# Expert products with phi, placed at the seam between a retention layer and two mixture-of-experts layers

## The chip, the cores and the metric

The kernel runs on one core of a Trainium2 chip. The metric is the device time of one execution in microseconds (us); lower is better. The engines are named as in the profile: PE multiplies matrices (PEld loads its weights), DVE, ACT and POOL work on vectors, and SP issues most of the transfers between the chip's memory (DRAM) and the on-chip memory (SBUF). Each engine works through its own instructions in order; semaphores tie them together. PE writes its results to PSUM, which has few banks.

## The reference

Three layers in float32. q, k and v have 4 batches, 8 heads, 768 steps and 64 columns, so the token matrix x is 3072 x 512.

```python
def _attn_ref(q, k, v):                       # retention
    for t in range(S):
        state = gamma * state + einsum('bhd,bhe->bhde', k[:, :, t], v[:, :, t])
        y[:, :, t] = scale * einsum('bhd,bhde->bhe', q[:, :, t], state)

def _moe_ref(x, w_gate, w_output_gate, w1, w2):   # each token goes to one of 8 experts
    e_idx = argmax(x @ w_gate, axis=1)
    for e in range(8):
        h = maximum(x[mask] @ w1[e], 0.0)
        out[mask] = gate_w[mask, None] * eom[mask, e, None] * (h @ w2[e])

def _moe2_ref(x, phi, w1, w2):                # 32 slots, 4 for each of 8 experts
    logits = x @ phi
    d = softmax(logits, axis=0)
    slot_input = d.T @ x
    slot_out[e] = maximum(slot_input[e] @ w1[e], 0.0) @ w2[e]
    return softmax(logits, axis=1) @ slot_out
```

## The kernel before

**Retention** goes over 24 tiles of 128 tokens (NTILE = 24), in steps i = 0 to 25. A step of the loop runs a fixed list of small stages, ORDER, in which each stage works on tile i, i-1 or i-2; the order of the list is the order of the instructions on every engine. It ends with the gate of each token: `run` counts tokens by expert, `count()` (step 25) sorts the experts by size into `ordi`, R0 to R4 and `im` (the tiles pa, pb and place_mm) place each token in its expert's list, and after the last step DVE makes from it `xidx`, the row numbers for gathering tokens, and `limi`, which says whether an expert has more tokens than its room. The scaled rows of x are written to DRAM as `xs`, 128 rows in a step.

**The products with phi.** The second layer needs only (h @ w2) @ phi of the first one's output for its logits, so w2 @ phi is made ahead for each expert: `wq(e)` multiplies the transposed second weight by phi. It has 16 matmuls, four (g = 0..3) for each of four k-quarters kk; the four of a quarter write 32 rows each of one PSUM bank. DVE transposes the bank into `ws`, and ACT's queue writes it to DRAM as `wps[e]`. The weights come in 32 loads `wt` of 512 KB on SP's queue (`wq_load`). A table, WAT, says in which step of retention the stage `wp` does which expert: 0 to 4 in steps 6, 10, 14, 18 and 22, and 5 in step 25 (NTILE + 1). Experts 6 and 7 follow after the last step, behind `limi` and the first `gather`. All use the one PSUM bank `xn`, which x's transposes use too.

**The block for left-over tokens.** All five engines read `limi` (line 632) and skip the block at line 739 if no expert overflows, as in this case. SBUF of retention and of this block is given to the experts' pools after it.

**The experts.** They come in order of size; "expert 0" is the first of them. `gather(e)` fetches its tokens (C[0] = 448 for expert 0, in tiles of 128 rows, XT) by four indirect transfers on POOL. `x_mm` transposes them on PE, for each k-quarter kk all token tiles; `x_split` makes of each quarter a rounded part xh (ACT) and the rest xl (DVE). `split_w(g)` does the same with the first weights (wh, wl), which `load_w(g)` loads as `r`. `l1(g)` is one of 8 column groups of an expert: 12 matmuls `hps`, then a relu on ACT. `behind(e - 1, f)` spreads the rest of the expert before over the groups. `logits(e, hf)` multiplies relu tiles by wps (loaded as `wp` by `load_wp`), its first half after group f = 4. `keep_warm` multiplies a tile by itself; nothing reads the result. `load_m2` fills a pool, `m2p`, with weights of the second layer, one tile of 256 KB in each group from the fifth on.

Of the kernel before, what the change touches and what calls it, by code (L numbers as in the profile page):

```python
# [9 lines left out]
F32 = mybir.dt.float32  # L10
# [12 lines left out]
E = 8  # L23
# [13 lines left out]
WAT = {6: 0, 10: 1, 14: 2, 18: 3, 22: 4, NTILE + 1: 5}  # L37
# [94 lines left out]
def retention_moe_kernel(ctx, tc, qt, kt, kn, vn, gates, moe_w1, moe_w2,  # L132
# [124 lines left out]
    with ExitStack() as pa:  # L257
# [43 lines left out]
        def wq(e):  # L301

            ps = pT.tile([128, 512], F32, tag="xn", name="wpsum")
            for kk in range(KD):
                t = wtt.pop((e, kk))
                for g in range(4):
                    nc.tensor.matmul(out=ps[32 * g:32 * g + 32, 0:256], lhsT=phi[:, kk, :], rhs=t[:, 256 * g:256 * g + 256],
                                     start=(kk == 0), stop=(kk == KD - 1), skip_group_check=True)
            ws = sc2.tile([128, KF, NS], F32, tag="ws", name="ws")
            nc.vector.transpose(out=ws, in_=ps[:, 0:256].rearrange("p (b t) -> p b t", t=32))  # L310
            nc.scalar.dma_start(out=wps[e].rearrange("p (f s) -> p f s", s=NS), in_=ws)

# [228 lines left out]
        def place_add(i):  # L541
# [11 lines left out]
            "oq": out_state, "os": out_scores, "st": state, "wp": lambda i: wq(WAT[i]) if i in WAT else None,  # L553
# [41 lines left out]
        for i in range(NTILE + 2):  # L595
            load(i + 3)
            load_dq(i + 2)
            if i == NTILE + 1:
                count()
            for n in ORDER:  # L600
                step[n](i)
            if i == 0:
                late_tables()
            for u in range(4 * E):
                if i == (1 + u if u < 20 else 21 + (u - 20) // 3):
                    wq_load(*divmod(u, 4))

        full = [128, E, 4, E]
# [14 lines left out]
        for e in range(6, E):  # L623
            wq(e)
# [126 lines left out]
    with ExitStack() as pb:  # L751
# [5 lines left out]
        xh, xl, hs, hB, wp, w2n, lps, lrs, lrs2, sms, lms, ces, gps, gsb, gts, slo = ({} for _ in range(16))  # L757
        puts = {}

        def x_mm(e, kk, pool=None, tag="x"):  # L760
            ps = (pool or ps_x).tile([128, C[e]], F32, tag=tag, name="xps")
            for j, r in enumerate(XT[e]):
                nc.tensor.transpose(out=ps[:, j * 128:j * 128 + r], in_=xg[e][j][0:r, kk * 128:(kk + 1) * 128],  # L763
                                    identity=ident[0:r, 0:r])
            return ps
# [10 lines left out]
        def keep_warm(w, n, pool, tag):  # L776

            ps = pool.tile([128, DM], F32, tag=tag, name="warm")
            for _ in range(n):
                nc.tensor.matmul(out=ps[:, 0:w.shape[1]], lhsT=w[:, 0:128], rhs=w, start=True, stop=True)  # L780
# [16 lines left out]
        def h_tr(e, f):  # L797

            c = C[e]
            if f == 0:  # L800
                hB[e] = hbp.tile([128, NBX, KF, 32], F32, tag="hB", name="hB")
            nc.vector.transpose(out=hB[e][:, 0:NB[e], f, :], in_=hs[e * KF + f][:, 0:c].rearrange("p (b t) -> p b t", t=32))  # L802

# [162 lines left out]
        split_w(1)  # L966
        keep_warm(w1_t[0][0], NW0, ps_h, "h")
        for kk, ps in enumerate([x_mm(0, kk, *((ps_x, "x") if kk < 2 else (ps_1, "lr"[kk - 2]))) for kk in range(KD)]):
            x_split(0, ps)
        for g in range(G):  # L970
            e, f = divmod(g, KF)
            if f == 0:
                if e + 1 < E:
                    gather(e + 1)
                load_er(e + 2)
                load_wp(e)
# [20 lines left out]
            if f == 4:  # L997
                logits(e, 0)
                mask(e)
# [215 lines left out]
```

## Time and profile before

| | us |
|---|---|
| median of 3 runs | 479.92 (477.62 to 480.44) |
| the profiled execution, its run | 484.3 |
| its span, first to last instruction | 482.5 |
| PE busy | 426.3 (88% of the span) |
| DVE busy | 279.4 (58%) |
| ACT busy | 165.8 (34%) |
| POOL busy | 110.1 (23%) |

The profile comes from one execution. Its times count from the span's start. Retention lasts to about 150, the experts run from about 159 to 395, and the second layer's own weights fill the rest. A busy PE is not always a PE at its peak, since matmuls overlap.

### The profile page before, as it was taken

What the parts mean: (1) busy time and instruction counts of PE and PEld (TensorE: products, weight loads), DVE (VectorE), ACT (ScalarE), POOL (GpSimd) and SP (SyncE); (2) the same over time, 40 slices, a digit from 0 to 9 for tenths busy, and PEclk for the clock granted to TensorE, in tenths of its full rate; (3) what the DMA queues carried; (4) which work ended last, traced back from release to release, by engine and by line L of the source; (5) the groups of instructions that cost most, each with busy time, mean ns of one, the idle gap of its engine ahead of it and who ended that gap; (6) DMA issues with size and microseconds to landing.
All of it is one profiled execution on the core that took longest, in us unless ns stands there. A gap on an engine that the chain in (4) does not pass through costs nothing.

```text
span 482.5 us, 12772 instructions
## 1 busy us (share of the span) xinstructions
PE 426.3 (88%) x4811; PEld 326.3 (68%) x4811; DVE 279.4 (58%) x964; ACT 165.8 (34%) x418; POOL 110.1 (23%) x113
## 2 busy tenths in 40 slices
PE   3899999989974799999999999998979989798874
PEld 3676777767742588876786778867767776425754
DVE  1797989888883326655555465654646636321433
ACT  1243334333340344534333344333343432110342
POOL 1712021211003311315133161241502112020040
PEclk9999999999999599999999999999999999989995
DMA  8999898898788457828839569397593945999998
GB/s 272 398 358 355 291 390 300 326 401 313 282 311 283 113 177 230 274 69 303 282 114 300 199 214 326 103 323 246 180 322 114 321 165 156 379 382 365 386 392 273
DMA packets 65176, 132.54 MB, mean 275 GB/s; under 512 B 8435, under 2 KB 16625, under 8 KB 65105
## 3 DMA queue, kind: packets, MB, share of 16 engines
q1 hardware_dynamic: 56848, 118.30, 70.0%
q0 software_dynamic: 3600, 9.05, 5.4%
q10 hardware_dynamic: 4656, 4.29, 2.7%
q8 instruction: 39, 0.64, 0.6%
q14 instruction: 33, 0.26, 0.2%
HBM read 117.58 MB, written 14.05 MB: 273 GB/s over the span
## 4 chain that ended last, share of the span: by engine, by line
PE 36%; DMA 13%; DVE 8%; issue 4%; ACT 3%; another core or an unknown queue 2%; ACTq 1%; SPq 0%; DVEq 0%
PE hps L790 16%; DMA r<-in_moe_w_dram 8%; PE gps L899 4%; DMA m<-in_moe_w_dram 3%; PE gsum L914 3%; DVE hB L802 2%; PE slo L923 2%; PE xps L763 2%; DVE wl L226 2%; PE lps L821 2%; PE fh L1057 2%; PE so L1107 2%; DVE xl L772 1%; ACT wh L225 1%
## 5 line engine op out<-in xcount | busy, mean ns | idle before, releaser
L790 PE MATMUL hps<-xh,wh 128*128 128x416 f32 (+2 forms) x256 | 96.1, 376 | 0.6 <-issue 0.6
L790 PE MATMUL hps<-xl,wh 128*128 128x416 f32 (+2 forms) x256 | 89.9, 351 | 0.7 <-issue 0.6
L790 PE MATMUL hps<-xh,wl 128*128 128x416 f32 (+2 forms) x256 | 89.5, 350 | 0.0
L226 DVE TENSOR_TENSOR wl<-r,wh 128x512 fp32r<-128x512 f32 x64 | 43.5, 680 | 55.9 <-ACT wh L225 52.1
L790 PEld LDWEIGHTS hps<-xh,wh 128*128 128x128 f32 x256 | 48.7, 190 | 14.8 <-issue 13.2
L795 ACT ACTIVATE h<-hps 128x416 f32<-128x416 f32 (+2 forms) x64 | 32.6, 509 | 74.3 <-PE hps L790 48.9
L225 ACT ACTIVATE wh<-r 128x512 fp32r<-128x512 f32 x64 | 40.3, 631 | 43.4 <-DMA r<-in_moe_w_dram 27.4
L790 PEld LDWEIGHTS hps<-xl,wh 128*128 128x128 f32 x256 | 48.9, 191 | 3.1 <-issue 2.1
L790 PEld LDWEIGHTS hps<-xh,wl 128*128 128x128 f32 x256 | 48.7, 190 | 1.2 <-issue 0.4
L882 POOL DMA_INDIRECT ctok<-cn,xidx x29 | 28.7, 990 | 88.3 <-DVE cn L879 81.9
L214 POOL DMA_INDIRECT xg<-xs,xidx x29 | 30.6, 1055 | 69.2 <-DMA wps<-ws 33.3
L346 POOL TENSOR_TENSOR k<-vk,cs 128x512 f32<-128x512 f32 x20 | 22.4, 1122 | 84.0 <-DMA vk<-in_vn_dram 48.3
L373 DVE TENSOR_TENSOR sS<-s,csa 128x512 f32<-128x512 f32 x48 | 30.7, 681 | 9.7 <-DMA csa<-in_consts_dram 8.1
L802 DVE STREAM_TRANSPOSE hB<-h 128x416 f32<-128x416 f32 (+2 forms) x64 | 34.3, 577 | 0.0
L830 POOL TENSOR_SCALAR lm<-cs,rt 128x416 f32<-128x416 f32 (+2 forms) x8 | 16.2, 2024 | 76.7 <-DVE srun L855 76.6
L363 PE MATMUL s<-qk 64*128 64x128 f32 x384 | 29.0, 292 | 4.3 <-DMA qk<-in_qt_dram 4.3
L363 PEld LDWEIGHTS s<-qk 64*128 64x128 f32 x384 | 24.3, 194 | 8.3 <-DMA qk<-in_qt_dram 4.3
L772 DVE TENSOR_TENSOR xl<-xps,xh 128x416 fp32r<-128x416 f32 (+2 forms) x32 | 18.3, 582 | 17.7 <-issue 8.7
L406 PE MATMUL o<-sS,vk 128*64 128x128 f32 x384 | 27.2, 281 | 0.2 <-DVE sS L373 0.2
L481 ACT ACTIVATE sm<-sm 128x8 f32<-128x8 f32 x24 | 5.1, 211 | 64.1 <-DVE sm L469 64.1
L899 PE MATMUL gps<-hB,pT 32*32 32x256 f32 x816 | 19.1, 384 | 8.4 <-DVE pT L853 8.4
L771 ACT ACTIVATE xh<-xps 128x416 fp32r<-128x416 f32 (+2 forms) x32 | 16.2, 513 | 19.2 <-PE hps L790 11.0
(155 smaller groups left out, 691.8 us busy)
## 6 DMA issues: line engine op xcount, KB each, us to landing
m<-in_moe_w_dram SPq DMA_DIRECT2D x128, 256.0 KB
wt<-in_moe_w_dram SPq DMA_DIRECT2D x32, 512.0 KB
r<-in_moe_w_dram SPq DMA_DIRECT2D x64, 256.0 KB
w<-in_moe_w_dram SPq DMA_DIRECT2D x64, 256.0 KB
vk<-in_vn_dram SPq DMA_DIRECT2D x12, 512.0 KB
qk<-in_kt_dram SPq DMA_DIRECT2D x12, 512.0 KB
xs<-xnat SPq DMA_DIRECT2D x24, 256.0 KB
qk<-in_qt_dram SPq DMA_DIRECT2D x11, 512.0 KB
```

The lines of the kernel that those rows point to most:

```text
L214: nc.gpsimd.indirect_dma_start(out=xg[e][j][0:r, :], out_offset=None, in_=xs[:, :], in_offset=bass.IndirectOffsetOnAxis(ap=xidx[0:r, e, j: ...
L225: nc.scalar.activation(out=hi, in_=t, func=ACTF.Copy)
L226: nc.vector.tensor_tensor(out=lo, in0=t, in1=hi, op=ALU.subtract)
L363: nc.tensor.matmul(out=ps[h][:, p, :], lhsT=raw["kt", i][r, p, :], rhs=raw["qt", i][r, p, :], start=True, stop=True, tile_position=(64 * h ...
L373: nc.vector.tensor_tensor(out=sS[i][:, :, h, :], in0=sps.pop((i, h)), in1=con("dm", 128).rearrange("p (a b) t -> p a b t", b=2)[:, :, h, : ...
L406: nc.tensor.matmul(out=o_at(i, p, h), lhsT=vv[:, 2 * p + h, :], rhs=s[:, p, h, :], start=(c == 0 and p < 2), stop=True, skip_group_check=True)
L772: nc.vector.tensor_tensor(out=lo[:, 0:c], in0=ps, in1=hi[:, 0:c], op=ALU.subtract)
L790: nc.tensor.matmul(out=ps, lhsT=a[:, kk * 128:(kk + 1) * 128], rhs=x[e][kk][:, 0:c], start=(n == 0), stop=(n == 11))
L795: nc.scalar.activation(out=hs[g][:, 0:c], in_=ps, func=ACTF.Relu)
L802: nc.vector.transpose(out=hB[e][:, 0:NB[e], f, :], in_=hs[e * KF + f][:, 0:c].rearrange("p (b t) -> p b t", t=32))
L882: put = nc.gpsimd.indirect_dma_start(out=ctok[:, :], out_offset=bass.IndirectOffsetOnAxis(ap=xidx[0:r, e, j:j + 1], axis=0), in_=cn[0:r, j ...
L899: nc.tensor.matmul(out=ps[a][32 * c:32 * c + 32, :], lhsT=pT_[q, b, :], rhs=hB[e][q, b].rearrange("p f t -> p (f t)"), start=(b < 4), stop ...
```

## The change

The products with phi of experts 5, 6 and 7 (the sixth to the eighth) move, and some work at the start of expert 0 is put in another order:

- Expert 5 is done in step 24, not 25. `wq` is split into `wq_mm` (matmuls) and `wq_put` (transpose and write). Expert 6 has its first two quarters in step 25, in a bank of the scores' tag `s`, its other two after the loop, and `wq_put(6)` after `limi` and the gather.
- Expert 7 is done in expert 0 of the first layer: eight loads of 256 KB go into the first tiles of `m2p` at its start, `phi_mm(0)` to `phi_mm(3)`, four matmuls each, follow the groups f = 1 to 4, and the last one transposes and writes.
- `load_wp(0)` is put behind `phi_mm(3)`, and `logits(0, 0)` and `mask(0)` after group 6 instead of 4.
- The `wt` loads of step 21 on come earlier by a step or so: two in step 20, three each in 21 and 22, none later.
- At the start of expert 0 `keep_warm` goes, x is transposed by token tile (all four quarters of a tile, then the next tile), and `split_w(1)` comes between x's second and third quarter.

```diff
-WAT = {6: 0, 10: 1, 14: 2, 18: 3, 22: 4, NTILE + 1: 5}
+WAT = {6: 0, 10: 1, 14: 2, 18: 3, 22: 4, NTILE: 5}
...
+        def wq(i):
+            if i in WAT:
+                wq_mm(WAT[i])
+                wq_put(WAT[i])
+            elif i == NTILE + 1:
+                wq_mm(6, range(2), "s")
...
-            for u in range(4 * E):
-                if i == (1 + u if u < 20 else 21 + (u - 20) // 3):
+            for u in range(4 * E - 4):
+                if i == (1 + u if u < 20 else 20 + (u - 19) // 3):
                     wq_load(*divmod(u, 4))
 
+        wq_mm(6, range(2, KD))
...
         gather(0)
-        for e in range(6, E):
-            wq(e)
+        wq_put(6)
...
+        def load_wt(kk):
+            for hf in range(2):
+                u = 2 * kk + hf
+                wtt[u] = m2p.tile([128, 512], F32, tag="m2", name="wt")
+                nc.sync.dma_start(out=wtt[u], in_=moe_w2[1, E - 1, kk * 32:(kk + 1) * 32, :].rearrange("a (b h f) -> (a b) h f", h=2, f=512)[:, hf])
+
+        def phi_mm(kk):
+
+            if kk == 0:
+                wpp[0] = ps_x.tile([128, 512], F32, tag="x", name="wpp")
+            for g in range(4):
+                nc.tensor.matmul(out=wpp[0][32 * g:32 * g + 32, 0:256], lhsT=phi[:, kk, :],
+                                 rhs=wtt[2 * kk + g // 2][:, 256 * (g % 2):256 * (g % 2) + 256],
+                                 start=(kk == 0), stop=(kk == KD - 1), skip_group_check=True)
+            if kk == KD - 1:
+                ws = sp.tile([128, KF, NS], F32, tag="wp", name="ws", bufs=2)
+                nc.vector.transpose(out=ws, in_=wpp[0][:, 0:256].rearrange("p (b t) -> p b t", t=32))
+                nc.scalar.dma_start(out=wps[E - 1].rearrange("p (f s) -> p f s", s=NS), in_=ws)
...
         split_w(0)
-        split_w(1)
-        keep_warm(w1_t[0][0], NW0, ps_h, "h")
-        for kk, ps in enumerate([x_mm(0, kk, *((ps_x, "x") if kk < 2 else (ps_1, "lr"[kk - 2]))) for kk in range(KD)]):
+        for kk in range(KD):
+            load_wt(kk)
+        xps = [(ps_x if kk < 2 else ps_1).tile([128, C[0]], F32, tag="xxlr"[kk], name="xps") for kk in range(KD)]
+        for j in range(len(XT[0])):
+            for kk in range(KD):
+                x_turn(0, kk, j, xps[kk])
+        for kk, ps in enumerate(xps):
             x_split(0, ps)
+            if kk == 1:
+                split_w(1)
...
-                load_wp(e)
+                if e:
+                    load_wp(e)
...
+            if e == 0 and 0 < f <= KD:
+                phi_mm(f - 1)
+                if f == KD:
+                    load_wp(0)
-            if f == 4:
+            if f == (4 if e else 6):
                 logits(e, 0)
                 mask(e)
```

PE in retention's steps 24 and 25 before, from the place search of step 24 (pb and pa) to the last products (wpsum); cp is the count, g the gate's bank:

```order
L538 MATMUL g<-pb,pa 128x32
L456 MATMUL xn<-cs_65,xT 128x128 x4
L569 LDWEIGHTS ones
L569 MATMUL cp<-run,ones 128x8
L502 LDWEIGHTS tri
L502 MATMUL g<-oh,tri 128x8
L503 LDWEIGHTS ones
L503 MATMUL g<-run,ones 128x8
L307 MATMUL wpsum<-wt,phi 32x256 x16
L538 MATMUL g<-pb,pa 128x32
L307 MATMUL wpsum<-wt,phi 32x256 x32
```

The same place now:

```order
L310 MATMUL wpsum<-wt,phi 32x256 x16
L551 MATMUL g<-pb,pa 128x32
L469 MATMUL xn<-cs_65,xT 128x128 x4
L582 LDWEIGHTS ones
L582 MATMUL cp<-run,ones 128x8
L515 LDWEIGHTS tri
L515 MATMUL g<-oh,tri 128x8
L516 LDWEIGHTS ones
L516 MATMUL g<-run,ones 128x8
L310 MATMUL wpsum<-wt,phi 32x256 x8
L551 MATMUL g<-pb,pa 128x32
L310 MATMUL wpsum<-wt,phi 32x256 x8
```

Expert 5's sixteen products stand a step earlier, ahead of step 24's place search; expert 6's stand in two halves around that of step 25; expert 7's are gone from here.

SP's queue at the start of the experts before (ordi is the number of an expert, wp the read of wps, r the first weights):

```order
L201 TENSOR_LOAD ordi
L201 ISA x2
L201 TENSOR_LOAD ordi
L201 ISA x2
L806 ISA
L806 DMA wp<-wps 128x256
L208 ISA
L208 DMA r_4494<-in_moe_w_dram 128x512
```

The same place now:

```order
L201 TENSOR_LOAD ordi
L201 ISA x2
L824 DMA wt<-in_moe_w_dram 128x512 x8
L201 TENSOR_LOAD ordi
L201 ISA x2
L208 ISA
L208 DMA r_4477<-in_moe_w_dram 128x512
```

And further on, where wp went, around the first load of the second layer's weights (m):

```order
L208 ISA
L208 DMA r_4574<-in_moe_w_dram 128x512
L246 DMA m_4576<-in_moe_w_dram 128x512
L841 ISA
L841 DMA wp<-wps 128x256
L208 ISA
L208 DMA r_4606<-in_moe_w_dram 128x512
L246 DMA m_4608<-in_moe_w_dram 128x512
```

The read wp left the head of the queue and stands behind the fifth r load of expert 0 and the first m; the eight wt loads stand at the head.

## Rows read from the trace of the kernel before

**Rows 1.** Chain of waits, 138 to 172: start us, us, what.
```profile
158.56 0.64 ACT wh L225
...
159.25 1.22 PE warm L780 x2
160.47 4.32 PE xps L763 x16
164.79 7.25 PE hps L790 x23
```

**Rows 2.** Windows around the seam: stretch, busy by engine, clock, DMA share, GB/s.
```profile
156.30:164.70 8.40, 5.46 (x18) 3.39 (x18) 2.97 (x5) 2.79 (x5) 0.36 (x1) 0.50 0.39 119
164.70:169.90 5.20, 5.20 (x15) 4.62 (x15) 1.42 (x3) 1.36 (x3) 4.13 (x5) 0.50 0.61 173
169.90:179.60 9.70, 9.70 (x48) 8.55 (x46) 2.77 (x4) 3.96 (x8) 1.23 (x1) 1.00 0.48 161
```

**Rows 3.** The tile limi: duration in ns min/median/max, first and last start.
```profile
L632 PEldq TENSOR_LOAD <-limi x1: 733/733/733, 151.3 to 151.3; - x1
...
L632 ACTq TENSOR_LOAD <-limi x1: 473/473/473, 153.7 to 153.7; - x1
```

**Rows 4.** Timeline, steps 24 and 25: start, us, engine, what, idle before and releaser.
```profile
139.07 0.69 ACT L495 ACTIVATE xnat<-xn,sm 128x512 f32<-128x512 f32 x1
...
139.69 0.29 DVE L526 TENSOR_SCALAR pa<-cs,sm 128x128 f32<-128x128 f32 x1
...
142.88 3.45 PE L307 MATMUL wpsum<-wt,phi 128*32 128x256 f32 x32 [0.66 <-ACT xnat L495]
...
146.41 0.45 DVE L310 STREAM_TRANSPOSE ws<-wpsum 128x256 f32<-128x256 f32 x1 [1.82 <-PE wpsum L307]
...
146.89 6.79 ACTq L311 DMA_DIRECT2D wps<-ws  x3
...
149.02 0.18 DVE L611 CAST xidx<-self 128x32 int32<-128x32 f32 x1
...
150.20 0.16 DVE L618 CAST limi<-lim 1x9 int32<-1x9 f32 x1
```

**Rows 5.** Source line 739, the end of the block: duration, first and last start.
```profile
L739 PEldq EVENT_SEMAPHORE  x2: 51/51/51, 156.6 to 156.7; - x2
...
L739 ACTq EVENT_SEMAPHORE  x2: 17/17/17, 158.4 to 158.5; - x2
...
L739 POOLq INC_SWDGE_SEM x1: 256/256/256, 159.7 to 159.7; - x1
```

**Rows 6.** Timeline of step 22, expert 4's products (x32: two passes each).
```profile
128.78 1.93 PE L307 MATMUL wpsum<-wt,phi 128*32 128x256 f32 x32
```

**Rows 7.** Timeline of POOL: the first and the last of four gather transfers.
```profile
150.68 1.25 POOL L214 DMA_INDIRECT xg<-xs,xidx  x1 [33.27 <-DMA wps<-ws]
...
154.86 0.96 POOL L214 DMA_INDIRECT xg<-xs,xidx  x1 [0.30 <-issue]
```

**Rows 8.** Timeline of PE in expert 0, around the first logits group.
```profile
179.11 0.37 PE L790 MATMUL hps<-xl,wh 128*128 128x448 f32 x1
179.32 0.37 PE L790 MATMUL hps<-xh,wl 128*128 128x448 f32 x1
179.61 0.96 PE L821 MATMUL lps<-h,wp 128*32 128x448 f32 x8
180.50 0.47 PE L790 MATMUL hps<-xh,wh 128*128 128x448 f32 x1
180.82 0.36 PE L790 MATMUL hps<-xl,wh 128*128 128x448 f32 x1
```

**Rows 9.** Timeline of SP's queue, 159 to 162.
```profile
160.04 0.94 SPq L208 DMA_DIRECT2D r<-in_moe_w_dram  x2
```

**Rows 10.** Windows after those loads; the last three are clock, DMA share, GB/s.
```profile
160.00:163.00 3.00, 3.00 (x13) 1.87 (x11) 1.14 (x2) 0.98 (x2) 0.00 (x0) 0.50 0.73 221
163.00:166.00 3.00, 3.00 (x10) 2.02 (x9) 1.85 (x4) 1.72 (x4) 1.36 (x2) 0.50 0.00 1
```

More of the change, by code (lines that the diff above doesn't have):

```diff
@@ L299, in wq_load, with wq_mm, wq_put @@
             nc.sync.dma_start(out=wtt[e, kk], in_=moe_w2[1, e, kk * 32:(kk + 1) * 32, :].rearrange("a (b f) -> (a b) f", f=FF))
-        def wq(e):
-            ps = pT.tile([128, 512], F32, tag="xn", name="wpsum")
-            for kk in range(KD):
+        wpsum = {}
+        def wq_mm(e, kks=range(KD), tag="xn"):
+            if kks[0] == 0:
+                wpsum[e] = pT.tile([128, 512], F32, tag=tag, name="wpsum", bufs=PB.get(tag, 1))
+            for kk in kks:
                 t = wtt.pop((e, kk))
                 for g in range(4):
-                    nc.tensor.matmul(out=ps[32 * g:32 * g + 32, 0:256], lhsT=phi[:, kk, :], rhs=t[:, 256 * g:256 * g + 256],
+                    nc.tensor.matmul(out=wpsum[e][32 * g:32 * g + 32, 0:256], lhsT=phi[:, kk, :], rhs=t[:, 256 * g:256 * g + 256],
                                      start=(kk == 0), stop=(kk == KD - 1), skip_group_check=True)
+        def wq_put(e):
             ws = sc2.tile([128, KF, NS], F32, tag="ws", name="ws")
-            nc.vector.transpose(out=ws, in_=ps[:, 0:256].rearrange("p (b t) -> p b t", t=32))
+            nc.vector.transpose(out=ws, in_=wpsum.pop(e)[:, 0:256].rearrange("p (b t) -> p b t", t=32))
             nc.scalar.dma_start(out=wps[e].rearrange("p (f s) -> p f s", s=NS), in_=ws)
+        def wq(i):
[4 more added lines that the diff above has]
+                wq_mm(6, range(2), "s")
         bds = [one.tile([128, 4, D], F32, name=f"bds{i}") for i in range(2)]
@@ L552, in retention_moe_kernel @@
             "xt": lambda i: x_trans(i - 1), "zk": lambda i: k_scale(i + 1), "zq": lambda i: q_scale(i + 1),
-            "oq": out_state, "os": out_scores, "st": state, "wp": lambda i: wq(WAT[i]) if i in WAT else None,
+            "oq": out_state, "os": out_scores, "st": state, "wp": wq,
         }
@@ L755, in retention_moe_kernel, with x_turn @@
         ps_1 = pb.enter_context(tc.tile_pool(name="ps_1", bufs=1, space=PSUM))
-        xh, xl, hs, hB, wp, w2n, lps, lrs, lrs2, sms, lms, ces, gps, gsb, gts, slo = ({} for _ in range(16))
+        xh, xl, hs, hB, wp, wpp, w2n, lps, lrs, lrs2, sms, lms, ces, gps, gsb, gts, slo = ({} for _ in range(17))
         puts = {}
+        def x_turn(e, kk, j, ps):
+            r = XT[e][j]
+            nc.tensor.transpose(out=ps[:, j * 128:j * 128 + r], in_=xg[e][j][0:r, kk * 128:(kk + 1) * 128], identity=ident[0:r, 0:r])
         def x_mm(e, kk, pool=None, tag="x"):
             ps = (pool or ps_x).tile([128, C[e]], F32, tag=tag, name="xps")
-            for j, r in enumerate(XT[e]):
-                nc.tensor.transpose(out=ps[:, j * 128:j * 128 + r], in_=xg[e][j][0:r, kk * 128:(kk + 1) * 128],
-                                    identity=ident[0:r, 0:r])
+            for j in range(len(XT[e])):
+                x_turn(e, kk, j, ps)
             return ps
```

## The prediction

> **What bounds the kernel now.** I read the chain of waits at the seam between retention and the experts, then the windows there, then every engine's rows around the conditional block, and last the PE rows of the first expert (expert 0 in the code). The chain over the seam is one line [rows 1]: ACT's first split wh, two warm matmuls, 16 transposes of x, then hps products without a break. Before it PE stands idle: in 156.3 to 164.7 it is busy 5.46 of 8.40 us, and the granted clock is 0.50, the 1.2 GHz level, until 169.9, 5.2 us after the first hps product; from then on PE is busy all the time at 1.00 [rows 2]. So at the seam each us by which the first hps product starts sooner counts in full, and in expert 0 each us given to PE costs in full.
>
> Why wh starts only at 158.56: ACT read limi, the number that decides the block, at 153.7 and PE at 151.3 [rows 3], though DVE had limi done at 150.20 + 0.16 [rows 4]. ACT had to issue the eighth expert's wps write first, and DVE to turn it. From its reading ACT needed 158.4 - 153.7 = 4.7 us to leave the block, PE 156.6 - 151.3 = 5.3 [rows 5].
>
> **Steps 24 and 25.** In step 25 DVE waited 1.82 us for the sixth expert's products and turned them in 0.45 [rows 4]; both stood ahead of xidx and limi and leave: about -2.2 (the turn overlaps its neighbours by 0.1). The products took 3.45 us there, at the lower clock, but 1.93 in step 22 at the full one [rows 6]. In step 24 they must wait for bank xn, which ACT frees at 139.07 + 0.69 = 139.76 [rows 4]; 1.93 us and 0.45 of turning put pa at 142.2 and not at 139.69 [rows 4]: +2.5. xidx and limi come 0.3 later: 149.5 and 150.7. The first half of the seventh expert's products (0.96 at full clock, a half of 1.93) lies on PE while DVE makes pa and pb; the second half runs while DVE makes xidx. Both are at nothing; without that cover the price is 1.9.
>
> **Leaving the block.** Now only the seventh's turn stands between limi and the read: DVE reads at 151.1, ACT at 151.5, PE at 150.8. With the times above ACT is out at 156.2, PE at 156.2, against 158.4 and 156.6.
>
> **Tokens and transposes.** The gather's first issue began at 150.68, its last ended at 154.86 + 0.96 = 155.8 [rows 7]. POOL releases its queue's counts at 159.7, after waiting for them to land [rows 5], so the last tile landed before 159.7; I take 159.4. The first issue stood 1.5 us after xidx (149.02 + 0.18), and the profile names a DMA as what it waited for [rows 4, 7]. The four loads that stood ahead of the last x rows in SP's queue are gone, so the gather starts 0 to 1.0 sooner; I take 0.5, last landing 158.9. Sixteen transposes take 4.32, 0.27 each [rows 1]. By token tile, eight run at 156.3 to 158.5 on tiles that have landed; the third tile then at 158.9 to 160.0, the fourth to 161.1. The first quarter of x is whole at 160.3, ACT's split of it takes about 0.6 (an estimate from the 0.64 of wh [rows 1]: 448 columns, not 512), the hand-overs between engines the rest, and hps starts near 161.2 instead of 164.79 [rows 1]: **-3.5**. Bounds: PE alone (no wait for tokens) 160.6, so -4.1; gather no earlier, 162.1, so -2.7. The warm matmuls (1.22 [rows 1]) vanish inside this; they ran at 0.50 and lifted nothing [rows 2].
>
> **Clock.** I leave its rise 5.2 us after the first hps product. A us at 0.50 loses half a us: if it rises three us sooner the sum gains 1.5; if it stays tied to 169.9 it loses another 1.7.
>
> **Eighth expert's products in expert 0.** Sixteen products in four groups, each between two hps groups on a PE that never idles. Nearest rows: the logits group, also four products of 32 output rows put among hps [rows 8]. The hps products follow at 0.205 us; from 179.32 to 180.82 pass 1.50 where two steps would take 0.41, so that group costs 1.09. It has 448 columns, ours 256: less 192 columns at 0.37 per 448, 0.16. I take 0.93, four times: **+3.7**. The lower end is 1.93 / 4 = 0.48 each [rows 6], products among their like: 1.9; the upper 1.09: 4.4. The row shows why the upper end is nearer: 0.29 us pass from the last hps start to the first logits start, where 0.205 is usual, and hps returns only as the group ends.
>
> The Trainium skill (TensorEngine Tiling (Array Packing), Key Properties) states that changing the tiling mode drains TensorE. By it each of the four groups pays twice and the sum takes the 3.7; without it, the 1.9. The trace agrees with the drain, by the 1.09.
>
> **The write and read of wps.** load_wp(0) now waits in SP's queue for the eighth write, made in expert 0. Let P be the end of the last phi product. DVE turns it (0.45 [rows 4]), ACT issues the write, it lands, SP issues the read, it lands. A quiet transfer took at most 2.4 us from its issue: the second r was issued near 160.6 [rows 9] and the engines moved nothing after 163.0 [rows 10]; that bounds a read from above. A write has no clean row: the gather's wait named the wps write issued at 146.89 and ended at 150.68, so at most 3.8 [rows 4, 7], under a full load. I take 2.4 for each: P + 0.5 + 2.4 + 0.3 + 2.4 = P + 5.6. Logits(0,0), put two groups later, is due at P + 24 x 0.205 = P + 4.9: a stall of 0.7. Behind load_wp on SP stands r of expert 1's first group, now issued at P + 3.7, landed at P + 6.1; its split stands on ACT ahead of a relu and of the splits of expert 1's x, each some 0.6, and ends a little later than due. Together **+0.9**; bounds 0 (transfers of 2.0) and 2.5 (a write of 3.8).
>
> The Trainium skill (DMA: Bandwidth & Descriptors, Anatomy of one DMA) gives about 2.0 us plus the bytes for a GpSimd DMA, most of it the receipt of the write. By it the two legs would be 2.3 us each, an estimate, and the stall 0.5. No run here shows such a write alone.
>
> **What else moves.** Eight loads (2 MB) leave retention for the start of expert 0. The first needs storage that the block frees, so it waits until POOL's release near 159.2 (0.5 before the 159.7); it can't collide with the first gather. Queued behind on SP: the next expert's number, r(3) to r(5). Eight issues at 0.47 [rows 9] put r(3) at 163.5; at 221 GB/s [rows 10] 2.4 MB land by 171, and it is due for l1(3) at about 171.4. It is hidden, by 0.4 us at that rate; SP's early loads are the cover. The second weight split put between x's second and third quarter, and mask(0) put two groups later, are at nothing: a quarter of x feeds three hps products, over 1 us at the lower clock, and a split takes 0.64 [rows 1]; POOL has no other work due. Without that cover the first costs 0.64. From expert 1 on each wait is tied to PE's progress, so the shift goes through to the end.
>
> **Sum.** -3.5 + 3.7 + 0.9 = +1.1 us on the profiled execution's span of 482.5 (its run is 484.3). The median of the three runs, 479.92, is 4.4 below that run; the same shift gives **481.0**. The gain is real but nearly all of it is handed back in expert 0.
>
> **Rivals.**
> First, phi products that cost what they cost among their like, and no stall: -3.5 + 1.9 = -1.6, 478.3. For it: the back-to-back row [rows 6]; against: the logits rows [rows 8]. With an earlier clock as well, -3.1, 476.8. Chance 0.26.
> Second, on the slower side: the round trip through DRAM is long. A write of 3.8 and r(8) behind it give 2.5 to 3.5 of stall, so -3.5 + 3.7 + 3.0 = +3.2, 483.1. It takes the forecast's place from a write plus read of about 6.5 us and passes 1% from about 8.7; the gather's wait [rows 7] speaks for it, the light load in expert 0 against. Chance 0.17.
> Third, the change doesn't shorten the seam: tokens land no earlier and the third and fourth tile are waited for until 159.7, and the clock keeps to 169.9: -2.7 + 1.7 + 3.7 + 0.9 = +3.6, 483.5. Chance 0.10.
> The forecast has 0.47, from 479.5 to 482.5.
>
> **How the numbers follow.** About 1%, 4.8 us, is what a measurement of this kernel can tell from no change. Faster by more needs the first rival with everything at its best end (-4.1 - 1.5 + 1.9 + 0): 0.05. Slower by more needs the second or third with another term at its bad end: 0.09. The rest, 0.86, is within. The range reaches half into the first rival and over the second and third's values: 477.2 to 484.2.
>
> **What would show it.** Right: limi near 150.7 and ACT's first wh near 156.3; hps from about 161.2, the clock at 1.00 some five us later; four phi groups that each add about 0.9 between hps groups; a wait of PE ahead of logits(0,0) under 1 us; the first logits group of expert 1 about 1 us later than now. Wrong: phi groups at 0.5; hps before 160.5; SP at load_wp(0) for over 5 us after the write's issue; a clock level that rises much sooner or later after the first product.

## The result and the profile after

| | before | after |
|---|---|---|
| median, us | 479.14 (4 runs, 477.62 to 480.44) | 485.27 (4 runs, 483.26 to 485.65) |
| ratio, 95% interval | | 1.0121 [1.0077, 1.0165] |
| the profiled execution: run, span | 484.3, 482.5 | 483.26, 481.5 |
| PE busy in it | 426.3 | 428.8 |

The change made the kernel slower by 1.2%. The forecast was 481.0 with a range to 484.2 and a chance of 0.09 for slower by more than 1%; the median lies above the range. The two traces don't show the loss as it is: the one of before is of an execution 5 us above that kernel's median, the one of after of the quickest of its four. Three more pairs were therefore measured, each on one chip: 1.0116 [1.0049, 1.0182], 1.0053 [1.0001, 1.0104] and 1.0061 [1.0021, 1.0101]. By the ratios that is 2.6 to 5.8 us. The kernel before, timed a second time against itself on the same three chips, came out at 0.9969, 1.0044 and 0.9993; so the pair of 1.0053 would not show a loss by itself, the four together do.

What the trace of after does show is where the seam's gain goes. First the seam, in its timeline (start us, us, engine, what, idle before and what ended it):

```profile
149.04 0.16 DVE L632 CAST limi<-lim 1x9 int32<-1x9 f32 x1
...
155.33 0.63 ACT L225 ACTIVATE wh<-r 128x512 fp32r<-128x512 f32 x1 [11.77 <-ACTq L752]
...
155.57 3.41 PE L775 MATMUL xps<-cs,xg 128*128 128x128 f32 x16 [7.01 <-PEq L752]
...
159.35 0.74 PE L806 MATMUL hps<-xh,wh 128*128 128x448 f32 x1 [0.37 <-ACT xh L787]
```

PE and ACT are out of the block together, the sixteen transposes take 3.41 us without a stop, and the first hps product starts 10.3 us after limi; before it was 14.5 (164.72 - 150.20 [rows 4]), by PE's timeline of before:

```profile
164.72 0.74 PE L790 MATMUL hps<-xh,wh 128*128 128x448 f32 x1
```

Then come the windows of expert 0 (us, busy time and count of PE, PEld, DVE, ACT and POOL, clock, DMA share, GB/s):

```profile
155.20:159.35 4.15, 3.41 (x17) 2.93 (x17) 0.72 (x2) 1.23 (x3) 0.86 (x1) 0.50 0.08 22
159.35:164.24 4.89, 4.89 (x12) 4.08 (x13) 3.39 (x6) 2.28 (x5) 3.82 (x5) 0.50 0.86 262
164.24:170.90 6.66, 6.39 (x41) 4.56 (x39) 0.00 (x0) 0.55 (x1) 1.24 (x1) 1.00 1.00 361
170.90:173.00 2.10, 0.90 (x4) 0.86 (x5) 1.09 (x2) 2.02 (x5) 0.00 (x0) 1.00 0.09 32
```

The clock is back at 1.00 4.9 us after the first product, as before (5.2) [rows 2]. But from 164.24 to 170.90 the DMA engines are full (1.00) and DVE and ACT do almost nothing: one relu in 6.7 us. ACT's timeline says what it waits for, SP's queue why:

```profile
164.47 0.55 ACT L811 ACTIVATE h<-hps 128x448 f32<-128x448 f32 x1 [2.83 <-PE hps L806]
170.99 0.63 ACT L225 ACTIVATE wh<-r 128x512 fp32r<-128x512 f32 x1 [5.97 <-DMA r<-in_moe_w_dram]
171.52 0.53 ACT L811 ACTIVATE h<-hps 128x448 f32<-128x448 f32 x1
171.94 0.62 ACT L225 ACTIVATE wh<-r 128x512 fp32r<-128x512 f32 x1
172.47 0.53 ACT L811 ACTIVATE h<-hps 128x448 f32<-128x448 f32 x1
```

```profile
158.53 4.52 SPq L824 DMA_DIRECT2D wt<-in_moe_w_dram  x8
163.91 9.74 SPq L208 DMA_DIRECT2D r<-in_moe_w_dram  x5
...
180.94 0.33 SPq L841 DMA_DIRECT2D wp<-wps  x1
181.50 0.33 SPq L208 DMA_DIRECT2D r<-in_moe_w_dram  x1
```

The eight `wt` loads start at 158.5, about a us after POOL lets go of the block (157.3 and 0.26 us more); r(3) is issued behind them at 163.9 (before: about 160 [rows 9]) and lands at 170.9, the longest of the `r` loads from 158 to 185, whose median is 2.7. The two views of after are line 752 and the tile r:

```profile
L752 POOLq INC_SWDGE_SEM x1: 256/256/256, 157.3 to 157.3; - x1
```

```profile
DMA to landing us min/median/max: 2.7/2.7/7.0
```

ACT works in order. It waits 5.97 us for r(3) with the relu of the second group behind it: that relu runs at 171.52, though the group's products ended near 166.9. PE has two banks for hps; the third group ends, and the fourth finds no bank free:

```profile
169.69 0.37 PE L806 MATMUL hps<-xh,wl 128*128 128x448 f32 x1
169.99 0.64 PE L831 MATMUL wpp<-wt,phi 128*32 128x256 f32 x8
172.10 0.47 PE L806 MATMUL hps<-xh,wh 128*128 128x448 f32 x1 [1.47 <-ACT h L811]
```

### The profile page after: what moved, and what is told of

It reads as the page before. It is cut to its first block, busy times and chain, and to the rows that moved or that the text cites. A ratio compares the mean times of both kernels' runs of the same rounds, so it can differ in the third digit from the quotient of the medians.

```text
span 481.5 us, 12781 instructions
## 1 busy us (share of the span) xinstructions
PE 428.8 (89%) x4809; PEld 326.9 (68%) x4809; DVE 276.5 (57%) x964; ACT 165.7 (34%) x418; POOL 110.4 (23%) x113
## 4 chain that ended last, share of the span: by engine, by line
PE 38%; DMA 17%; DVE 4%; ACT 3%; SPq 2%; issue 2%; ACTq 1%; another core or an unknown queue 1%
DMA r<-in_moe_w_dram 15%; PE hps L806 14%; PE gps L934 5%; PE fh L1103 3%; PE slo L958 3%; PE gsum L949 3%; PE so L1153 3%; PE xps L775 2%; PE lps L856 2%; ACT wh L225 1%; DMA w<-in_moe_w_dram 1%; DVE wl L226 1%; DMA m<-in_moe_w_dram 1%; SPq L824 1%; ACTq L1213 1%
## 5 line engine op out<-in xcount | busy, mean ns | idle before, releaser
L359 POOL TENSOR_TENSOR k<-vk,cs 128x512 f32<-128x512 f32 x20 | 22.3, 1114 | 83.8 <-DMA vk<-in_vn_dram 46.3
L386 DVE TENSOR_TENSOR sS<-s,csa 128x512 f32<-128x512 f32 x48 | 30.8, 683 | 10.6 <-DMA csa<-in_consts_dram 8.6
L934 PE MATMUL gps<-hB,pT 32*32 32x256 f32 x816 | 23.1, 468 | 10.9 <-DVE pT L888 10.9
L775 PEld LDWEIGHTS xps<-cs,xg 128*128 128x128 f32 (+1 forms) x116 | 14.3, 150 | 18.0 <-issue 8.8
L934 PEld LDWEIGHTS gps<-hB,pT 32*32 32x32 f32 x816 | 14.1, 113 | 17.4 <-issue 11.9
```

Source lines behind the costliest of these rows:

```text
L386: nc.vector.tensor_tensor(out=sS[i][:, :, h, :], in0=sps.pop((i, h)), in1=con("dm", 128).rearrange("p (a b) t -> p a b t", b=2)[:, :, h, : ...
L934: nc.tensor.matmul(out=ps[a][32 * c:32 * c + 32, :], lhsT=pT_[q, b, :], rhs=hB[e][q, b].rearrange("p f t -> p (f t)"), start=(b < 4), stop ...
```

## The experiments

Theory 1: the loss is in expert 0, in the phi products and above all in the loads that come late behind `wt` and `load_wp(0)` on SP. Theory 2: it is in later stretches in which the clock is granted at 0.50, after PE's waits in the later experts, which a different arrival moves.

For every kernel I read four moments from its timeline: limi, the first hps product, the first relu, and the relu of expert 1's first group. Three intervals follow, in us: the seam (limi to hps), expert 0 (first relu to expert 1's first), and both with the clock's rise between them (limi to expert 1). They don't depend on how long retention took. Ratios are against before on the same chip. The kernels stand in five sets, each measured on a chip of its own; a set's first row has the median of its before in brackets.

| kernel | ratio [95%] | median (before) | limi to hps | expert 0 | limi to expert 1 |
|---|---|---|---|---|---|
| before, first trace | | | 14.5 | 23.6 | 43.0 |
| after, first trace | 1.0121 [1.0077, 1.0165] | 485.27 (479.14) | 10.3 | 28.1 | 43.6 |
| e0_before | 0.9969 [0.9926, 1.0013] | 477.55 (477.66) | 14.6 | 23.4 | 42.8 |
| e1_after | 1.0116 [1.0049, 1.0182] | 481.74 | 10.0 | 28.1 | 43.1 |
| e2_wt_late | 1.0039 [0.9992, 1.0086] | 480.72 | 10.1 | 26.4 | 40.1 |
| e3_wp_late | 1.0072 [1.0027, 1.0116] | 481.25 | 10.1 | 26.9 | 42.2 |
| b2_before | 1.0044 [0.9988, 1.0101] | 484.22 (484.30) | 14.1 | 23.1 | 40.9 |
| a2_after | 1.0053 [1.0001, 1.0104] | 486.13 | 10.2 | 32.2 | 46.0 |
| e4_both_late | 1.0020 [0.9970, 1.0069] | 483.04 | 10.4 | 26.3 | 41.4 |
| e5_after_fill | 1.0103 [0.9982, 1.0225] | 486.26 | 10.5 | 27.9 | 43.0 |
| e6_move_only | 1.0010 [0.9972, 1.0048] | 487.49 (486.20) | 12.0 | 27.7 | 44.6 |
| e7_seam_only | 0.9882 [0.9840, 0.9923] | 480.74 | 12.4 | 23.4 | 39.5 |
| e8_x_only | 0.9856 [0.9802, 0.9910] | 480.23 | 11.5 | 23.3 | 40.0 |
| e9_phi_once | 0.9924 [0.9883, 0.9966] | 483.48 | 10.0 | 25.1 | 38.8 |
| b3_before | 0.9993 [0.9963, 1.0024] | 478.42 (478.12) | 14.0 | 23.4 | 41.5 |
| a3_after | 1.0061 [1.0021, 1.0101] | 482.53 | 10.2 | 28.8 | 43.9 |
| e10_loads_only | 1.0029 [0.9998, 1.0060] | 479.93 | 11.2 | 25.4 | 41.1 |
| e11_seam_again | 0.9947 [0.9913, 0.9981] | 475.24 | 11.3 | 23.3 | 39.2 |
| e12_x_again | 0.9931 [0.9896, 0.9966] | 475.82 (478.30) | 13.0 | 23.2 | 41.3 |
| e13_x_bank | 0.9920 [0.9890, 0.9950] | 474.68 | 10.6 | 23.4 | 38.4 |

**First set: the two kernels and one kind of late load each.** In e2_wt_late the `wt` loads stand two behind each of r(3) to r(6); in e3_wp_late `load_wp(0)` stands behind r(8).

```diff
-        for kk in range(KD):
-            load_wt(kk)
...
                 load_w(g + 3)
+                if g < KD:
+                    load_wt(g)
```

```diff
                 load_w(g + 3)
+                if g == 5:
+                    load_wp(0)
...
-                if f == KD:
-                    load_wp(0)
```

> The kernel before, unchanged, for a trace taken on the same chip as the others: ratio 1.000, about 479 to 480 us. The trace shown of before is of an execution of 484.3, above its own timed runs; if the 6 us of the result is real work of the change, this trace is shorter than that one, by 4 us or so, in stretches where the changed kernel is not.

> The changed kernel, unchanged, for a trace beside that of before on one chip: about 485, ratio 1.012. Theory 1 (late loads): the time is lost where ACT waits for r(3), about 6.0 us of ACT's wait and 1.5 of PE's, and for r(8), and is visible as a difference of the relu times in expert 0 and 1. Theory 2 (clock): the relu times of the two kernels are within 1 us of each other after expert 1, and the difference arises in later stretches in which the changed kernel shows a granted clock of 0.50 and the kernel before does not; each stretch of 3.4 us at that level costs 1.7.

> The eight loads of the eighth expert's weights stand behind r(3) to r(6) in SP's queue, two behind each, and not ahead of r(3). Theory 1 (r(3) late behind 2 MB): ACT's wait of 6.0 us for r(3) goes, PE's 1.47 behind it too, and the lead of 5.1 at the first relu is kept up to the phi groups: 3 to 5 us less than the changed kernel, about 481, ratio 1.002 to 1.006. Theory 2 (clock in later stretches): expert 0 ends sooner by 1.5 to 4, but the end moves by under 1 us. Third, the loads then come too late for the phi groups: PE waits at them, and the time is as it was or worse.

> load_wp(0) stands behind r(8) in SP's queue, not ahead of r(8). Theory 1: r(8) and r(9), issued at 181.5 and 182.6 with load_wp ahead, come 2 to 3 us sooner, and the 1.1 us lost between the third and fourth relu group from the end of expert 0 goes: 1 us less than the changed kernel. The rival: load_wp itself is then later and PE waits for it ahead of the logits, no gain or 1 us worse. Theory 2 (clock): no change at the end.

The loss is real on one chip, and expert 0 takes 28.1 us where it took 23.4. Moving the `wt` loads behind r(3) takes 1.7 us off expert 0, and moving `load_wp(0)` 1.2; of this 1.2, 0.6 falls between the eighth group and expert 1, where `load_wp(0)` was in the way, and some 0.4 is a shorter wait of PE for r(3) (0.8 us, 1.2 in e1_after). Both ratios fall, and the first comes near 1, but their intervals overlap that of e1_after. Theory 2 had something for it too: the trace of e1_after has stretches at 0.50 in experts 6 and 7, that of e0_before one in expert 5.

**Second set: repeats, both kinds of loads late, and a filled wait.** e4_both_late joins the two edits. e5_after_fill lets PE work while it waits for the gate products of experts 2 to 7:

```diff
             elif f == 4:
+                if e:
+                    keep_warm(ident, 4, ps_1, "l")
                 slot_h(e)
```

> The kernel before again, for a second trace of a quick execution: ratio 1.00. In its traces so far PE waits 1.4 to 2.0 us for the gate products (gps) in each of the sixth to eighth expert and the granted clock drops to 0.50 for 3.4 us after none or one of these waits. If the drops are what tells the kernels apart, none or one is seen here in experts 5 to 7.

> The changed kernel again, for a third trace: ratio about 1.012. Theory 1 (late loads): the lead of the first relu is 5.0 to 5.7 us, 1.5 after expert 0 and 0.8 after expert 1, as in its two traces. Theory 2 (clock): a wait of 1.9 to 2.6 us for gps in experts 6 and 7 and behind each a stretch of 3.4 us at 0.50, which costs 1.3 to 1.4 in the time between two relu groups, as in all traces of the changed kernel so far.

> The changed kernel with four small matmuls, whose result nobody reads, put on PE ahead of the gate products in experts 2 to 7, where PE waits for DVE's turned rows anyway. Theory 2 (clock): the drops to 0.50 after those waits go, relu time between the fourth and eighth group of experts 6 and 7 falls from 15.6-16.0 to 14.5-14.7 each, and the time is 2.5 to 3 us less than the changed kernel's. Theory 1: these drops are not where the difference lies; the time stays within 1 us of the changed kernel.

> Both kinds of loads late: the eight loads of the eighth expert's weights two behind each of r(3) to r(6), and load_wp(0) behind r(8). Theory 1: PE no longer waits in expert 0 for r(3) or r(8); the lead after expert 0 is 3 us or more, and the time 2 to 4 us under the changed kernel's. Theory 2: the end moves by less than 1 us, since later waits for the weight stream and the drops of the clock decide it.

b2_before has one stretch at 0.50 in experts 5 to 7, as its expectation allows; but a2_after, for which two were expected, has only one too, and also in expert 7. Here are the two, before first:

```profile
389.60:393.00 3.40, 3.40 (x79) 1.45 (x70) 1.72 (x6) 1.09 (x3) 1.38 (x1) 0.50 0.45 148
```

```profile
392.70:396.10 3.40, 3.40 (x103) 1.64 (x71) 1.89 (x7) 0.66 (x3) 1.68 (x1) 0.50 0.50 159
```

So on this chip the stretches don't tell the two kernels apart. On the chip of the fourth set it is the trace of before that has more of them in experts 1 to 7, three against one. With the fill the waits shrink (PE's waits from 190 to 405 in a2_after, then in e5_after_fill: us in total, times, longest), and no stretch at 0.50 is left in experts 1 to 7:

```profile
PE gps L934 <- DVE pT L888: 7.9, 6, 2.2
```

```profile
PE gps L934 <- DVE pT L888: 3.4, 4, 1.1
```

From the fourth to the last relu of expert 7, 14.6 us pass and not 16.0. The time doesn't show it, 486.26 beside 486.13, but e5_after_fill was timed only four times and its interval, 1.2% to either side, is wider than the gain of 0.5 to 0.6% that was looked for. What speaks against theory 2 as the explanation of the loss is the count of the stretches; a small share of it stays possible. In e4_both_late PE no longer waits for a relu; this is all that it waits for in 160 to 195, and expert 0 takes 26.3 us:

```profile
PE hps L806 <- ACT xh L787: 0.4, 1, 0.4
```

What is left over before, 2.9 us, are the products. a2_after shows the loads at their worst: its first relu came early, at 161.22, since the clock was at 1.00 from the first product on, and the whole lead went into a wait for r(3) of 7.8 us:

```profile
169.56 0.63 ACT L225 ACTIVATE wh<-r 128x512 fp32r<-128x512 f32 x1 [7.79 <-DMA r<-in_moe_w_dram]
```

PE stood still for 3.3 us, and its clock then fell back to the 1.2 GHz level (a2_after's windows):

```profile
164.20:169.50 5.30, 3.19 (x20) 2.25 (x20) 0.00 (x0) 0.00 (x0) 0.00 (x0) 1.00 1.01 356
169.50:170.80 1.30, 0.13 (x1) 0.13 (x2) 0.58 (x1) 1.24 (x3) 0.00 (x0) 1.00 0.09 33
170.80:174.20 3.40, 3.40 (x10) 3.05 (x11) 1.50 (x3) 1.29 (x3) 0.00 (x0) 0.50 0.54 151
```

**Third set: the parts alone.** e6_move_only is before with the eighth expert's products, loads, `load_wp(0)` and `logits(0, 0)` moved as in the change; e7_seam_only is the changed kernel without that move; e8_x_only is before with only x by token tile, the second weight split between x's quarters and no warm products; e9_phi_once is e4_both_late with all phi products in one run.

The core of e7_seam_only, then of e9_phi_once:

```diff
         wq_put(6)
+        wq_mm(7)
+        wq_put(7)
...
-        for kk in range(KD):
-            load_wt(kk)
...
-            if e == 0 and 0 < f <= KD:
-                phi_mm(f - 1)
```

```diff
-            if e == 0 and 0 < f <= KD:
-                phi_mm(f - 1)
+            if e == 0 and f == KD:
+                for kk in range(KD):
+                    phi_mm(kk)
```

> The kernel before with one part of the change alone: the eighth expert's products in expert 0, with their eight loads, load_wp(0) behind them and logits(0,0) two groups later. Retention, the seam's order of x and the warm products are as before. Theory 1 (the moved products and what their loads delay cost more than they free): between the first relu and expert 1's first, 28 to 32 us against 23.4 of before; at the seam the eighth expert's turn and write no longer stand ahead of ACT's reading of limi, which frees 1 to 2 us; in sum 3 to 6 us slower than before, ratio 1.006 to 1.012. Rival: the loss comes from the other parts, and this part alone is within 1 us of before.

> The changed kernel without that part: the eighth expert's products and write stand at the seam again, behind those of the seventh, and expert 0 has no phi groups, no wt loads and load_wp(0) at its start. Theory 1: between the first relu and expert 1's first 23.4 us as in the kernel before, hps from about 160 to 162, 2 to 4 us under the kernel before at the first relu, and the end 2 to 3 us under it: ratio 0.994 to 0.997. Theory 2 (a lead is eaten later, by the weight stream or by the clock, whatever made it): the lead is there after expert 0 and gone by the end, ratio 1.000 or above.

> The kernel before with only x turned by token tile in expert 0, no warm products, and the second weight split between x's second and third quarter. ACT leaves the block as late as before, at about 158.5, so x's tiles have landed by then: hps starts sooner by the 1.2 us of the warm products at most, at about 163.5. Ratio 0.997 to 1.000. If a lead of 1 us is kept to the end, theory 2 is wrong for small leads.

> The changed kernel with both kinds of loads late (as e4_both_late) and all sixteen phi products of expert 0 in one run behind the fourth group, not four groups. If a group pays for standing alone among hps products (0.76 each where four in a row among their like take 0.48), the sixteen take 2.0 to 2.2 here and not 3.0: 23.4 + 2.1 = 25.5 us between the first relu and expert 1's first, against 26.3 in e4_both_late. Time 1 us under e4_both_late: ratio 0.998 to 1.001. If each product has its price wherever it stands, 26.3 as there.

In e6 the seam gives 2.3 us and expert 0 takes 4.3 more: the move alone loses 2 us by its trace. Its ratio, 1.0010 [0.9972, 1.0048], shows no loss and misses the expected 1.006 to 1.012. e7 and e8, run again on other chips, came out 0.7% higher there, so ratios of this set are best compared among themselves: e6 lies 1.3% over e7, which has the rest of the change without the move. Without the move (e7) the change is faster than before, and so is the order of x by itself (e8), by more than expected. e9 shows that a group of phi products pays for standing alone: with sixteen in a row hps goes on after 2.06 us (174.38 - 171.91 less two steps of 0.205) and expert 0 takes 25.1 us, not 26.3. PE's timeline in e9_phi_once:

```profile
171.91 0.37 PE L806 MATMUL hps<-xh,wl 128*128 128x448 f32 x1
172.21 1.93 PE L831 MATMUL wpp<-wt,phi 128*32 128x256 f32 x32
174.07 0.47 PE L806 MATMUL hps<-xh,wh 128*128 128x448 f32 x1
174.38 0.36 PE L806 MATMUL hps<-xl,wh 128*128 128x448 f32 x1
```

**Fourth set: the loads' price by itself, on one chip with both kernels.** e10_loads_only is e7_seam_only with the eight `wt` loads where the change has them; nothing reads them.

```diff
         split_w(0)
+        for kk in range(KD):
+            load_wt(kk)
```

> The kernel before, for a trace on the same chip as the three that follow: 23.1 to 23.6 us between the first relu and expert 1's first, about 14 us from limi to the first hps product. Ratio 1.000.

> The changed kernel on the same chip: 10.0 to 10.4 us from limi to the first hps product, 28 to 32 us between the first relu and expert 1's first (the later the first relu lies ahead of r(3)'s landing at about 170, the more). Ratio 1.005 to 1.012. If the sum of these two differences explains the time, the relu times of expert 1 differ between the kernels by about what the times differ by, within 1 to 2 us.

> The kernel of e7_seam_only (the eighth expert's products at the seam) with the eight loads of 256 KB put where the changed kernel has them, ahead of r(3) on SP; nothing reads them. Theory 1: the loads alone make ACT wait for r(3), to about 169 to 171; between the first relu and expert 1's first 25 to 28 us, not 23.4, and the time 2 to 5 us above e7_seam_only's. Rival: the loads are hidden as forecast, and the loss of expert 0 is the products' alone: 23.4 us and the time of e7_seam_only within 1 us.

> The kernel of e7_seam_only again, beside the changed kernel on one chip: 23.4 us between the first relu and expert 1's first. Theory 1: ratio 0.985 to 0.995. Rival (the gain of its first run was that chip's): within 0.5% of before.

This is the decisive pair. ACT's timeline without the loads (e11_seam_again), then with them (e10_loads_only):

```profile
167.74 0.55 ACT L813 ACTIVATE h<-hps 128x448 f32<-128x448 f32 x1 [1.42 <-PE hps L808]
168.18 0.62 ACT L225 ACTIVATE wh<-r 128x512 fp32r<-128x512 f32 x1
170.22 0.55 ACT L813 ACTIVATE h<-hps 128x448 f32<-128x448 f32 x1 [1.42 <-PE hps L808]
```

```profile
167.16 0.55 ACT L813 ACTIVATE h<-hps 128x448 f32<-128x448 f32 x1 [2.20 <-PE hps L808]
172.84 0.63 ACT L225 ACTIVATE wh<-r 128x512 fp32r<-128x512 f32 x1 [5.14 <-DMA r<-in_moe_w_dram]
173.38 0.53 ACT L813 ACTIVATE h<-hps 128x448 f32<-128x448 f32 x1
```

Without the loads ACT waits for PE, as it should; with them for r(3), 5.14 us, PE 1.9 us for ACT, and expert 0 takes 25.4 us, not 23.3. By the ratios the seam's part gives 0.5% (1.0 - 0.9947), the loads take 0.8% (1.0029 - 0.9947, some 3.9 us, with intervals of 0.3% each) and the rest of the move 0.3%, which is within the intervals. Two things limit this price. Expert 0 shows 2.1 of the 3.9 us; where the rest arises isn't shown. And e10_loads_only moves 2 MB more than e11_seam_again (134.66 MB and 132.56), whereas the change takes the eight loads out of retention; so 0.8% is not quite what they cost in the changed kernel. b3_before and a3_after differ by 4.7 us at expert 1's first relu (190.62 and 195.34), and the medians by 4.1. Of these 4.7, though, 2.3 had arisen by limi (149.10 and 151.40), and over four traces of each kernel limi comes no later in the changed one (147.4 to 151.4, and 148.0 to 150.2); so that part is of these two executions.

**Fifth set: is the move needed?** In e13_x_bank the eighth expert's products get a bank of their own, so that they don't wait for the turn of the seventh's, and ACT reads limi sooner without any move.

```diff
-        for e in range(6, E):
-            wq(e)
+        wq(6)
+        wq(7, "s")
```

> The kernel of e8_x_only (before, with x turned by token tile and no warm products) on another chip: from limi to the first hps product 11.5 us against 14 to 14.6 of before, 23.4 us in expert 0 as before, and so 2.5 to 3 us under before at expert 1's first relu. If that lead is kept, ratio 0.993 to 0.996; if its first ratio, 0.986, was for the larger part that chip's, near 0.995; if the gain is given back later, 1.000.

> e12_x_again with the eighth expert's products in a bank of the scores' tag, so that they follow the seventh's and don't wait for DVE's turn of these behind limi. DVE turns the eighth's some 2 us sooner, ACT issues its write and reads limi 2 us sooner; PE's own way out of the block (4.1 to 5.2 us from its reading) then bounds: limi to the first hps product 10 to 10.5 us, not 11.5, and the time 1 us under e12_x_again. If the landing of the tokens bounds, no change.

The order of x keeps 0.7% on a second chip; the 1.4% of its first run was in part that chip's. Its trace, of the longest of its twelve executions, misses the expected 11.5 us from limi to hps (13.0): ACT was out of the block 9.3 us after limi, in e8_x_only 7.8. DVE's turn of the eighth expert's products came 0.4 us later than there; the rest is open. The bank takes limi to hps down to 10.6 us, nearly the 10.2 of the changed kernel. PE is out of the block 6.4 us after limi, as in the changed kernel (6.5), and then its transposes wait for tokens, so that they take 3.9 us and not 3.4 (e13_x_bank):

```profile
157.42 1.94 PE L762 MATMUL xps<-cs,xg 128*128 128x128 f32 x8 [5.12 <-ACTq L739]
...
159.58 1.73 PE L762 MATMUL xps<-cs,xg 128*128 128x128 f32 x8 [0.21 <-DMA xg<-xs,xidx]
```

At 0.992 [0.989, 0.995] it is faster than before, and so than the changed kernel, which was slower. The bank's own share isn't shown by the times (0.9931 without it, 0.9920 with it); that the seam's gain was to be had without the move is shown by limi to hps, in one trace.

## Why the prediction was wrong, step by step

**The seam (-3.5): right, a little better.** The forecast put hps 10.5 us after limi (161.2 - 150.7); four traces of the changed kernel show 10.0 to 10.3, four of before 14.0 to 14.6: -4.1. PE's transposes don't wait for the third token tile, and by token tile they take 3.41 us, not 4.32. The +0.3 for a later limi can't be seen: limi lies at 147.4 to 151.4 in the changed kernel and at 148.0 to 150.2 in before.

**The clock (5.2 us after the first product): right in this trace by chance.** It is 4.9 here, 2.3 in b2_before and 3.0 in b3_before, and in a2_after, e2_wt_late, e7_seam_only and e9_phi_once the clock is at 1.00 before the first product. So the rise isn't tied to that product; from it to the first relu pass 3.6 to 5.2 us, a spread of 1.6 that the forecast priced (1.5 for three us) but kept out of its sum.

**The phi groups (+3.7): somewhat less.** From 166.50 to 167.67 pass 1.17 us between hps starts where 0.41 is usual:

```profile
166.50 0.37 PE L806 MATMUL hps<-xh,wl 128*128 128x448 f32 x1
166.79 0.64 PE L831 MATMUL wpp<-wt,phi 128*32 128x256 f32 x8
167.36 0.47 PE L806 MATMUL hps<-xh,wh 128*128 128x448 f32 x1
167.67 0.36 PE L806 MATMUL hps<-xl,wh 128*128 128x448 f32 x1
```

So a group costs 0.76, four 3.0; e4_both_late, where nothing waits, gives 2.9 in all (26.3 - 23.4). The logits row [rows 8] was the right neighbour; the forecast was 0.17 a group too high. Sixteen in a row cost 2.06 (e9_phi_once), a fixed price of some 0.3 for each visit. The Trainium skill (TensorEngine Tiling (Array Packing), Key Properties) says that a change of tiling mode drains TensorE; the difference between one visit and four (2.06 and 3.0) agrees with that.

**The eight wt loads ("hidden, by 0.4 us"): this is the step that failed.** The landing of r(3) was forecast for 171 and came at 170.9, but that is luck: limi came 1.7 us sooner in this trace than the forecast had it (149.04, not 150.7). Counted from limi, the forecast has r(3) issued at 12.8 us, landed at 20.3 and due at 20.7. (The 171.4 of the due time stands there without its working.) The four traces of the changed kernel miss both ends:

- It lands late. r(3) is issued 14.3 to 15.4 us after limi, and its split on ACT starts 21.3 to 22.2 after it. The first `wt` load starts at 9.5 to 9.8 and not at 8.5, and behind the eighth 1.4 to 2.1 us pass until r(3) is issued, not 1.0. From issue to landing it takes 7.0 us in the trace of after, 0.5 less than forecast, at 361 GB/s and not 221 and with more bytes queued.
- It is due sooner. Had its split started by 18.9 to 20.5 us after limi, PE would not have waited. PE's fourth group needs that split (0.63 us), and it needs a bank, which the relu of the second group frees. That relu was ready at 166.9 but stands behind the split in ACT's queue. The relu's own share is at most 0.5 of the 1.47 us (from the split's end at 171.62 to 172.10), since the fourth group reads the split's result itself. For r(8) the forecast did name the relu behind the split; for r(3) it did not.

So a wait put at nothing was 1.2 to 1.9 us of PE in three traces, and in a2_after 3.3 with some 1.5 more for the clock that fell behind it, 4.9 in all. The loads alone make 2.1 (e10_loads_only, 25.4 - 23.3). r(3) follows limi and not the products: in the eight traces that have the loads ahead of it, its split starts 21.1 to 22.3 us after limi, while hps starts 10.0 to 12.0 after it. So what PE gains ahead of the fourth group, by the seam or by an earlier clock, is waited away, up to the 32.2 us of a2_after.

**The write and read of wps (+0.9): right.** From the first product of the eighth group to that of expert 1's first group 3.8 us pass in before, and 3.8 where `load_wp(0)` stands behind r(8) (e3_wp_late, e4_both_late); in the four traces of the changed kernel 4.3, 4.4, 4.8 and 4.5, so +0.5 to +1.0, and 4.1 in e2_wt_late. The way is the one that the forecast named behind `load_wp(0)`: the splits of r(8) and r(9) wait for their loads, and the splits of expert 1's x stand behind them (after; ACT and two rows of PE):

```profile
184.29 0.63 ACT L225 ACTIVATE wh<-r 128x512 fp32r<-128x512 f32 x1 [2.52 <-DMA r<-in_moe_w_dram]
...
185.74 0.47 PE L806 MATMUL hps<-xh,wh 128*128 128x448 f32 x1
...
186.83 0.63 ACT L225 ACTIVATE wh<-r 128x512 fp32r<-128x512 f32 x1 [1.47 <-DMA r<-in_moe_w_dram]
187.37 0.91 ACT L787 ACTIVATE xh<-xps 128x416 fp32r<-128x416 f32 x2
...
190.04 0.46 PE L806 MATMUL hps<-xh,wh 128*128 128x416 f32 x1
```

PE never waits ahead of logits(0, 0); the stall of 0.7 forecast there isn't seen.

**"From expert 1 on each wait is tied to PE's progress": these traces can't tell.** From expert 1's first relu to expert 7's last the eight traces of the two kernels take 206.8 to 214.7 us, with no order between the kernels. Part of that is the chip: in b2_before and a2_after relus at the experts' starts wait some 3 to 4 us (here a2_after, the relu of expert 2's first group), which e1_after doesn't show, and the first trace of before has it, that of after not.

```profile
227.04 0.52 ACT L811 ACTIVATE h<-hps 128x416 f32<-128x416 f32 x1 [3.91 <-remote]
```

**The sum.** Forecast: -3.5 + 3.7 + 0.9 = +1.1, with r(3) at nothing. By the four traces: seam -4.1, products +2.9, wps +0.5 to +1.0, r(3) +1.2 to +4.9; trace by trace +0.6 to +4.7, 1.9 on average. The ratios give 2.6 to 5.8, 4.2 on average. The four ends that the traces show lie only 0.5 us apart on average, since the traced executions of before mostly lie above its medians, those of after mostly below. So r(3) is what the forecast lacked in expert 0, and some 2 us of the loss, about half, stay open. Later stretches at 0.50 were tried (e5_after_fill) and neither account for it nor are ruled out.

One thing in the traces may bear on the open half, though none shows how often it happens. In before, an early rise of the clock brings expert 1 sooner: 40.9 and 41.5 us after limi (b2_before, b3_before) and not 42.8 to 43.0. In the changed kernel it brings it later, since the lead is waited away and the clock falls again: 46.0 (a2_after) and not 43.1 to 43.9.

**The rivals.** The second and third had the right sign by the wrong mechanism: neither the wps round trip nor a seam that stays long. A late r(3) was dismissed for a cover of 0.4 us, and no rival carried it. With a wait of 1.2 to 4.9 us, as measured, a rival of its own would have stood at 482.2 to 485.9, around the median of 485.27.

## What to carry to other kernels

When you say that a load is hidden, count its landing and its due time from one event that both follow (here limi); two clock times from one trace can agree by luck. Go back from the products to the first engine that uses the load, and look what stands behind that use in its queue. Work moved to a stage where PE is the bound pays its full price, and its loads push back the queue they join; a cover of a few tenths of a us is a rival, not a cover. Before a move is bought for what it frees at another place, try whether that can be freed by itself, as a second bank seems to do here.

## What the runs showed of the hardware

Four products of 32 output rows among full ones cost 0.76 us a visit, sixteen in one visit 2.06. In a2_after a PE that stood still for 3.3 us at full clock was granted 0.50 for the 3.4 us after; a stand of 1.47 in the first trace of after was not followed by this. Relus at the experts' starts wait some 3 to 4 us longer on two chips than on three others, so two traces can be compared by their ends only if they come from one chip.
